# Two slots of SMELU moved to VectorE and GpSimd, one PSUM bank and one output pair moved, loads issued later

## The chip, the cores and the metric

The kernel runs on one core of one Trainium2 chip. The metric is the device time of one execution in microseconds (us). Before the change the median of three runs is 313.86 us (313.83 to 314.38). The profiled execution has a span of 311.6 us from its first to its last instruction.

## What is computed

Sliding-window attention over 8 batches of 8 heads with 576 positions and head size 64, and behind it a two-layer network of 4608 tokens with the activation SMELU between the layers:

```python
scores = scale * np.matmul(q, k.transpose(0, 1, 3, 2))
mask = np.abs(pos[:, None] - pos[None, :]) <= 32
attn = softmax(np.where(mask, scores, -1e9))
x = (attn @ v).transpose(0, 2, 1, 3).reshape(B * S, H * D)     # 4608 x 512
h = x @ w_in                                                   # 4608 x 2048
g = np.where(h >= 1, h, np.where(h <= -1, 0.0, (h + 1) ** 2 / 4))
out = g @ w_out                                                # 4608 x 512
```

So SMELU is zero below -1, the identity above 1, and a quarter of the square of h + 1 between.

## The kernel before

Inputs are float32 in memory and bfloat16 on chip; the sums are float32. Tokens of the network are taken in 18 tiles of 256, and the 2048 hidden columns in 8 blocks of 256. One **slot** `a` of the main loop (L470) is one block of one tile: `t, f = divmod(a, 8)`. In a slot TensorE multiplies `xT` (the transposed output of attention) by a block of `w_in`: 8 matmuls into a tile `hp` of PSUM, 128 partitions by 512 floats, one bank (L492). SMELU of it goes to `gT`, which holds the activations of a tile. Eight slots later blocks of the second layer follow from `gT` and `w_out`: early on in units called `pair` (L440: 8 matmuls of width 256, in an order given by the list `pairs` of slot and unit), later `quarter` (L425: 4 matmuls of width 512).

Attention is spread over the same slots by the table `ev`: transposes of q and k (`tposes`, L323), scores with exponential (`scores`, L211), products with v and the row sums (`sums`, L265). The sums end with two activations on ScalarE and a multiplication on VectorE, which writes `xT`. These multiplications are put off to the next call of `flush`, which comes ahead of and behind SMELU in the next slot (L481, L505). Slot 8 is the first of the second tile of tokens: it reads the columns of `xT` that the multiplications after slots 3, 4 and 5 write (L305 and L308).

The order of work on each engine is that of the program (`manual_schedule`, L73), each engine works its queue in order, and waits between engines go by semaphores that the tile framework places. A tile of a pool with two buffers waits until the last reader of the tile before the last has finished.

**PSUM.** Four pools share the eight banks. `ps_h` has two one-bank buffers for `hp`; `ps_o` has two one-bank buffers for outputs (`op`); `ps_s` and `ps_n` have two banks each for attention. In slots 6 and 7 `hp` is taken from `ps_o` (L486). The buffers of `ps_o` go round: slot 6's `hp`, the output of pairs 0 to 3, then slot 7's `hp`, which so takes the bank of slot 6's. In `ps_h` the tile of slot 8 follows those of slots 4 and 5.

**SMELU** has two forms, both beginning with r = max(0, (h + 1) / 2) on ScalarE (`rr`, L496). In most slots VectorE computes mx = max(h, r) and then g = min(r, 1) * mx (L503, L504). In the slots of `two_on_act` ScalarE also squares r, and VectorE computes g = min(max(h, 1), r squared) (L500, L501). Slots 4 and 5 have the first form.

**Loads.** All loads but the very first go through GpSimd's queue in program order: those of the first batch and `w_in`, the masks' copies, the first half of `w_out` (256 of its 512 columns), then q, k and v of the second batch (`load_rows`, L88; `load_v`, L101), the second half of `w_out`, and q, k and v of the third. A load waits there until the load eight before it has landed. The second batch's q and k are first read by `tposes` in slots 11 and 12 (L412), its v in slot 14. Later batches are loaded by slots (L415 to L421).

**Pairs.** `pairs` puts pair 5, which reads the activations of slots 10 and 11, into slot 13. Slot 12 transposes k of the second batch, ScalarE and VectorE copy it to `kT`, and slot 13 computes scores from that, then pair 5, then the scores of position 13.5.

Of the kernel before, what the change touches and what calls it, by code (L numbers as in the profile page):

```python
# [9 lines left out]
AF = mybir.ActivationFunctionType  # L10
ALU = mybir.AluOpType
# [3 lines left out]
def kernel(  # L15
# [49 lines left out]
    bias = const.tile([128, 192], BF, name="bias")  # L65
# [8 lines left out]
    V, P, A = nc.vector, nc.gpsimd, nc.scalar  # L74
# [19 lines left out]
    def load_nat(b, t):  # L94
        src, dst, nm = ((q, qn, "qn"), (k, kn, "kn"))[t]
        x = dst[b] = nat.tile([128, NU, 2, D], BF, name=nm, tag=nm)
        for h in range(2):
            nc.gpsimd.dma_start(out=x[:, :, h], in_=src[b, NY * h:NY * h + NY].rearrange("y s d -> (y s) d")  # L98
                                .rearrange("(u p) d -> p u d", p=128))

    def load_v(b, n):  # L101
        if b not in vn:
            vn[b] = nat.tile([128, 2 * NC, 2, D], BF, name="vn", tag="vn", bufs=3)
        h, a = divmod(n, 2)
        y = NY * h + 2 * a
        nc.gpsimd.dma_start(out=vn[b][64 * a:64 * a + 64, :, h], in_=v[b, y:y + 2].rearrange("y s d -> (y s) d")  # L106
                            .rearrange("(c r) d -> r c d", r=64))
# [34 lines left out]
    def put(todo):  # L142
        for fn, *x in todo:
            fn(*x)
# [7 lines left out]
    for m, n, x in ((mask4, 8, 128), (mask8, 4, TAIL)):  # L152
        P.tensor_copy(m.rearrange("p (n j) -> p n j", n=n),
                      band[:, :x].rearrange("p (n j) -> p n j", n=1).to_broadcast([128, n, x]))
    put([(load_w_out, 0, 4, 8), (load_w_out, 0, 8, 16)] + [(load_rows, 1, t) for t in range(2)])
    put([(load_v, 1, n) for n in range(4)] + [(load_w_out, 1, 8 * n, 8 * n + 8) for n in range(2)])
    put([(load_rows, 2, t) for t in range(2)] + [(load_v, 2, n) for n in range(4)])


    kT = {}  # L160
# [31 lines left out]
    def xpose(b, t):  # L192

        nc.sync.dma_start_transpose(out=qkT(b, t).rearrange("d (u p) -> d u p", p=128),
                                    in_=(qn, kn)[t][b].rearrange("p u h d -> p (u h d)"))
# [115 lines left out]
    def flush():  # L311
        while muls:
            muls.pop(0)()
# [61 lines left out]

    NB = NT // TB
    NF = DFF // 256
    pairs = [(6, 0), (8, 1), (9, 2), (10, 3), (11, 4), (13, 5), (15, 6), (15, 8), (16, 7), (17, 9)]
    two_on_act = (1, 7, 8, 9, 10, 11, 12)
    ev = {}  # L380

# [34 lines left out]
    for b in range(LONG, B):  # L416
        a = sl[5 * (b - 1) - 7] - 17
# [39 lines left out]
    def run(pos):  # L457
        todo = []
        for fn, *x in ev.get(pos, []):
            if fn is sums:  # L460
                todo.append(sums(*x))
            elif fn is tposes:
                tposes(*x)
            else:
                pool = (x.pop(),) if x[-1] in (ps_s, ps_n, ps_o) else ()
                fn(*x, eng, *pool)
        for end in todo:
            end()

    for a in range(NF * NB + NF):  # L470
        t, f = divmod(a, NF)
        eng = None if a < 14 else V
        post = [x for n, x in pairs if n == a] + [a - NF] * (a >= 2 * NF + 2)
        for b, x in loads.get(a, []):
            if x < 2:
                load_nat(b, x)
            else:
                for n in range(4):
                    load_v(b, n)
        if a == 0 or a > 3:  # L480
            flush()  # L481
        if t < NB:
            if t not in gT:
                gT[t] = gtp.tile([128, 2 * NF, TB], BF, name="gT", tag="gT")
            r0 = TB * t % RING
            if a in (6, 7):  # L486
                hp = ps_o.tile([128, 2, TB], FP, name="hp", tag="op")
            else:
                hp = ps_h.tile([128, 2, TB], FP, name="hp", tag="hp")
            for j in range(2):  # L490
                for n, kk in enumerate((0, 2, 1, 3)):
                    nc.tensor.matmul(hp[:, j], w_in[:, kk, 256 * f + 128 * j:256 * f + 128 * j + 128],  # L492
                                     xT[:, kk, r0:r0 + TB], start=n == 0, stop=n == 3)

            rr = ewp.tile([128, 2, TB], FP, name="rr")
            A.activation(rr, hp, AF.Relu, scale=0.5, bias=0.5)  # L496
            g = gT[t][:, 2 * f:2 * f + 2]
            mx = ewp.tile([128, 2, TB], FP, name="mx")
            if a in two_on_act:
                A.activation(mx, rr, AF.Square)  # L500
                V.scalar_tensor_tensor(g, hp, 1.0, mx, op0=ALU.max, op1=ALU.min)  # L501
            else:
                V.tensor_max(mx, hp, rr)  # L503
                V.scalar_tensor_tensor(g, rr, 1.0, mx, op0=ALU.min, op1=ALU.mult)  # L504
        flush()  # L505
        run(a)
        for x in post:
            (pair if x < 4 * 4 else quarter)(x)
        run(a + 0.5)
        for x in xps.get(a, []):  # L510
            xpose(*x)
# [30 lines left out]
```

The softmax here doesn't subtract the row's maximum and nothing guards it: scores larger than these inputs give would overflow.

## Time and profile before

| what | from the profile |
|---|---|
| span | 311.6 us, 8569 instructions |
| TensorE matmuls, first layer (L492) | 149.3 us, 273 ns each |
| TensorE matmuls, second layer (L432, L448) | 123.0 and 16.5 us |
| SMELU on ScalarE (L496) | 85.7 us, 595 ns each |
| SMELU on VectorE (L503, L504) | 94.5 and 95.3 us, 690 and 696 ns each |
| GpSimd | 73.5 us, nearly all of it issuing loads |
| chain that ended last, by engine | PE 91%, DVE 3%, ACT 3%, issue 3% |
| granted TensorE clock | 0.998 of full speed |

PE is TensorE, PEld its weight loads, DVE VectorE, ACT ScalarE, POOL GpSimd, SP SyncE. L492 is line 492 of the kernel. In a timeline a row gives the start, the duration, engine, line, operation, output and inputs, and in brackets how long the engine sat idle before it and what released it; "x8" is a run of eight instructions. A matmul's recorded duration holds its passage through the array, and the next starts before it ends: eight matmuls of width 256 in a row take 0.87 us in the chain of waits. Engines that are often idle cost nothing unless TensorE waits for them.

### The profile page before, as it was taken

To read this page: it belongs to the slowest core of one execution; us is meant where nothing else is said; L and a number is where in the kernel's file an instruction comes from. 1 tells how busy PE (TensorE), PEld (TensorE's weight loads), DVE (VectorE), ACT (ScalarE), POOL (GpSimd) and SP (SyncE) were. 2 spreads that over 40 slices of the span, in tenths; PEclk is the share of its full clock that TensorE was granted. 3 is DMA by queue.
4 is the path that set the end of the run, shared out by engine and by line. 5 is a ranking of instruction groups with operands and counts; after the bars stand their busy time and mean duration, and the time that the engine had idled before them with its cause. 6 is when DMAs were issued, how large, how long until landed. Compare 5 with 4: busy or idle time off the path is not lost.

```text
span 311.6 us, 8569 instructions
## 1 busy us (share of the span) xinstructions
PE 297.6 (95%) x3669; PEld 207.2 (66%) x3706; DVE 244.9 (79%) x381; ACT 195.3 (63%) x323; POOL 73.5 (24%) x89
## 2 busy tenths in 40 slices
PE   8997989999999999999999999999999999999995
PEld 3566868886666666666666666666666666666652
DVE  4287558888888888888888888888888888888760
ACT  3686876776765766567656666566676666554431
POOL 8898344643061223040504000000000000000000
PEclk9999999999999999999999999999999999999999
DMA  9999999999999999597998592005501100110111
GB/s 151 183 198 199 175 214 177 173 164 167 168 176 131 112 187 162 62 112 153 160 95 81 65 154 70 34 36 113 111 34 36 37 34 36 37 36 34 52 51 67
DMA packets 124118, 34.54 MB, mean 111 GB/s; under 512 B 108208, under 2 KB 119728, under 8 KB 124080
## 3 DMA queue, kind: packets, MB, share of 16 engines
q0 software_dynamic: 94736, 18.06, 75.5%
q1 hardware_dynamic: 29200, 15.63, 20.9%
q8 instruction: 29, 0.48, 0.6%
q10 hardware_dynamic: 144, 0.29, 0.3%
q14 instruction: 9, 0.07, 0.1%
HBM read 36.70 MB, written 9.44 MB: 148 GB/s over the span
## 4 chain that ended last, share of the span: by engine, by line
PE 91%; DVE 3%; ACT 3%; issue 3%; ACTq 0%
PE hp L492 39%; PE op L432 35%; PE bb L293 6%; PE op L448 4%; PE bb L227 2%; PE z L336 2%; PE tp L187 1%; DVE kT L190 1%; DVE xT L305 1%; ACT rc L300 1%; DVE mx L503 1%; ACT rr L496 1%; ACT lr L299 1%; DVE gT L501 0%; ACT mx L500 0%
## 5 line engine op out<-in xcount | busy, mean ns | idle before, releaser
L492 PE MATMUL hp<-xT,w_in 128*128 128x256 bf16 x1152 | 149.3, 273 | 2.8 <-DVE mx L503 1.9
L496 ACT ACTIVATE rr<-hp 128x512 f32<-128x512 f32 x144 | 85.7, 595 | 88.3 <-PE hp L492 88.2
L492 PEld LDWEIGHTS <-w_in 128*128 128x128 bf16 x1152 | 111.9, 98 | 42.5 <-issue 3.3
L432 PE MATMUL op<-w_out,gT 128*128 128x512 bf16 x477 | 123.0, 379 | 5.1 <-issue 4.9
L503 DVE TENSOR_TENSOR mx<-hp,rr 128x512 f32<-128x512 f32 x137 | 94.5, 690 | 31.8 <-ACT rr L496 29.6
L504 DVE SCALAR_TENSOR_TENSOR gT<-rr,mx 128x512 bf16<-128x512 f32 x137 | 95.3, 696 | 4.7
L432 PEld LDWEIGHTS <-gT 128*128 128x128 bf16 x512 | 47.5, 98 | 36.8
L235 ACT ACTIVATE pt<-bb 128x1024 bf16<-128x1024 f32 (+1 forms) x33 | 32.8, 1002 | 5.3 <-PE bb L227 3.8
L106 POOL DMA_DIRECT2D vn<-in_v_dram x32 | 27.3, 868 | 34.1 <-PE bb L227 31.5
L305 DVE TENSOR_TENSOR xT<-bb,rc 128x512 bf16<-128x512 f32 (+1 forms) x32 | 21.1, 658 | 10.1 <-ACT rc L300 9.6
L437 ACT COPY osb<-op 128x512 f32<-128x512 f32 x32 | 18.6, 583 | 11.5 <-PE op L432 11.1
L300 ACT ACTIVATE rc<-lr 128x512 f32<-128x512 f32 (+2 forms) x40 | 23.5, 587 | 1.3
L98 POOL DMA_DIRECT2D qn<-in_q_dram x10 | 12.2, 1221 | 43.5 <-DMA qT<-qn 37.5
L299 ACT ACTIVATE lr<-bb 128x512 f32<-128x512 f32 (+2 forms) x40 | 22.0, 551 | 0.2 <-PE bb L293 0.2
L201 DVE TENSOR_TENSOR pt<-pt,mask 128x1024 bf16<-128x1024 bf16 (+1 forms) x33 | 20.3, 614 | 0.0
L293 PE MATMUL bb<-pt,ones 64*64 64x256 bf16 (+3 forms) x352 | 19.5, 255 | 0.1
L293 PE MATMUL bb<-pt,vn 64*64 64x128 bf16 (+3 forms) x712 | 18.4, 204 | 0.0
L293 PEld LDWEIGHTS <-vn 64*64 64x64 bf16 x712 | 16.7, 107 | 0.2 <-DMA vn<-in_v_dram 0.2
L448 PE MATMUL op<-w_out,gT 128*128 128x256 bf16 x128 | 16.5, 273 | 0.0
L293 PEld LDWEIGHTS <-ones 64*64 64x64 bf16 x352 | 10.2, 105 | 8.5 <-issue 8.4
L98 POOL DMA_DIRECT2D kn<-in_k_dram x10 | 12.1, 1213 | 10.7 <-DMA kT<-kn 3.9
L227 PE MATMUL bb<-qT,kT 64*64 64x128 bf16 (+1 forms) x520 | 13.1, 217 | 0.4 <-DVE kT L190 0.4
(56 smaller groups left out, 118.7 us busy)
## 6 DMA issues: line engine op xcount, KB each, us to landing
out_dram<-osb SPq DMA_DIRECT2D x36, 256.0 KB, 2.3
vn<-in_v_dram POOLq DMA_DIRECT2D x32, 144.0 KB, 8.8
qn<-in_q_dram POOLq DMA_DIRECT2D x10, 288.0 KB, 7.2
kn<-in_k_dram POOLq DMA_DIRECT2D x10, 288.0 KB, 8.0
w_in<-in_moe_w_in_dram POOLq DMA_DIRECT2D x12, 128.0 KB, 5.6
w_out<-in_moe_w_out_dram POOLq DMA_DIRECT2D x3, 512.0 KB, 15.5
qn<-in_q_dram POOLq DMA_DIRECT2D x2, 576.0 KB, 12.8
kn<-in_k_dram POOLq DMA_DIRECT2D x2, 576.0 KB, 13.9
```

What stands on the lines that cost most here:

```text
L98: nc.gpsimd.dma_start(out=x[:, :, h], in_=src[b, NY * h:NY * h + NY].rearrange("y s d -> (y s) d") .rearrange("(u p) d -> p u d", p=128))
L106: nc.gpsimd.dma_start(out=vn[b][64 * a:64 * a + 64, :, h], in_=v[b, y:y + 2].rearrange("y s d -> (y s) d") .rearrange("(c r) d -> r c d", ...
L235: A.activation(p, ps[:, :, :w * n].rearrange(like, y=m), AF.Exp, scale=D ** -0.5)
L293: nc.tensor.matmul(bb[HD[h], a, o + c0:o + c1], ones[HD[a]] if c is None else vn[b][HD[a], c, h], p(a, h), start=n == 0, stop=True, skip_g ...
L299: A.activation(lr[:, :, :D0], bb[:, :, D0:2 * D0], AF.Ln)
L300: A.activation(rc[:, :, :D0], lr[:, :, :D0], AF.Exp, scale=-1.0)
L432: nc.tensor.matmul(o, gT[tt // 2][:, j, 128 * (tt % 2):128 * (tt % 2) + 128], w_out[:, j], start=not done, stop=len(done) == 2 * NF - 1, s ...
L448: nc.tensor.matmul(o[:, tt], gT[p][:, j, 128 * tt:128 * tt + 128], w_out[:, j, 256 * half:256 * half + 256], start=not done, stop=len(done ...
L492: nc.tensor.matmul(hp[:, j], w_in[:, kk, 256 * f + 128 * j:256 * f + 128 * j + 128], xT[:, kk, r0:r0 + TB], start=n == 0, stop=n == 3)
L496: A.activation(rr, hp, AF.Relu, scale=0.5, bias=0.5)
L503: V.tensor_max(mx, hp, rr)
L504: V.scalar_tensor_tensor(g, rr, 1.0, mx, op0=ALU.min, op1=ALU.mult)
```

## The change

Three things. Slot 7's `hp` comes from `ps_h` again, so that it no longer waits for slot 6's bank. Pair 5 goes from slot 13 to slot 12, behind the transposes of k. And slots 4 and 5 compute SMELU without ScalarE: VectorE takes max(h, -1) + 1 from PSUM, GpSimd halves it in place and squares it, and VectorE ends as in the second form. The loads of the second and third batch and of the second half of `w_out`, which stood in GpSimd's queue ahead of the main loop, are issued from slot 4 (q) and slot 5 (all others), each behind GpSimd's two operations of that slot. The aim is to take work off ScalarE in those slots, to take away two waits of TensorE, and to keep the loads in GpSimd's queue from standing ahead of its arithmetic.

```diff
-    put([(load_w_out, 0, 4, 8), (load_w_out, 0, 8, 16)] + [(load_rows, 1, t) for t in range(2)])
-    put([(load_v, 1, n) for n in range(4)] + [(load_w_out, 1, 8 * n, 8 * n + 8) for n in range(2)])
-    put([(load_rows, 2, t) for t in range(2)] + [(load_v, 2, n) for n in range(4)])
+    put([(load_w_out, 0, 4, 8), (load_w_out, 0, 8, 16)])
+    later = {4: [(load_rows, 1, 0)], 5: [(load_rows, 1, 1)] + [(load_v, 1, n) for n in range(4)]}
+    later[5] += [(load_w_out, 1, 8 * n, 8 * n + 8) for n in range(2)]
+    later[5] += [(load_rows, 2, t) for t in range(2)] + [(load_v, 2, n) for n in range(4)]
...
-    pairs = [(6, 0), (8, 1), (9, 2), (10, 3), (11, 4), (13, 5), (15, 6), (15, 8), (16, 7), (17, 9)]
+    pairs = [(6, 0), (8, 1), (9, 2), (10, 3), (11, 4), (12, 5), (15, 6), (15, 8), (16, 7), (17, 9)]
...
-            if a in (6, 7):
+            if a == 6:
                 hp = ps_o.tile([128, 2, TB], FP, name="hp", tag="op")
...
             rr = ewp.tile([128, 2, TB], FP, name="rr")
-            A.activation(rr, hp, AF.Relu, scale=0.5, bias=0.5)
             g = gT[t][:, 2 * f:2 * f + 2]
             mx = ewp.tile([128, 2, TB], FP, name="mx")
-            if a in two_on_act:
+            if a in later:
+                V.tensor_scalar(rr, hp, -1.0, 1.0, op0=ALU.max, op1=ALU.add)
+                P.tensor_scalar(rr, rr, 0.5, None, op0=ALU.mult)
+                P.tensor_mul(mx, rr, rr)
+                V.scalar_tensor_tensor(g, hp, 1.0, mx, op0=ALU.max, op1=ALU.min)
+                put(later[a])
+            else:
+                A.activation(rr, hp, AF.Relu, scale=0.5, bias=0.5)
+            if a in later:
+                pass
+            elif a in two_on_act:
                 A.activation(mx, rr, AF.Square)
                 V.scalar_tensor_tensor(g, hp, 1.0, mx, op0=ALU.max, op1=ALU.min)
```

## The prediction

> **What bounds the kernel now.** The first page gives each engine's share: TensorE is busy 95% of the span, VectorE 79%, ScalarE 63%. A mean hides stages, so next comes the table of stages, cut at 23.6, 45 and 280 us (columns: length, then busy time of PE, PEld, DVE, ACT, POOL, granted clock, DMA share, GB/s):
>
> ```profile
> PE 297.6 (95%) x3669; PEld 207.2 (66%) x3706; DVE 244.9 (79%) x381; ACT 195.3 (63%) x323; POOL 73.5 (24%) x89
> ...
> 23.60:45.00 21.40, 18.61 (x278) 15.25 (x267) 13.55 (x21) 16.09 (x28) 11.83 (x16) 1.00 1.64 194
> 45.00:280.00 235.00, 230.08 (x2890) 162.20 (x2919) 201.40 (x306) 153.32 (x255) 41.08 (x40) 1.00 0.98 105
> ```
>
> From 45 to 280 us TensorE is busy 98% and no wait of over 0.2 us for another engine shows, so a microsecond won or lost on TensorE before 45 us reaches the end whole. All the edits act between 23.6 and 45 us, where TensorE is idle 2.8 us. The waits of TensorE from 20 to 45 us (total, times, longest) name it:
>
> ```profile
> PE hp L492 <- DVE mx L503: 1.9, 1, 1.9
> PE bb L206 <- DVE kT L190: 0.6, 1, 0.6
> PE bb L227 <- DVE kT L190: 0.2, 1, 0.2
> ```
>
> The first is slot 7, as the timelines of VectorE and TensorE show (start, duration):
>
> ```profile
> 24.09 0.62 DVE L305 TENSOR_TENSOR xT<-bb,rc 128x448 bf16<-128x448 f32 x1 [0.54 <-ACT rc L300]
> 24.63 0.68 DVE L503 TENSOR_TENSOR mx<-hp,rr 128x512 f32<-128x512 f32 x1
> 25.35 0.69 DVE L504 SCALAR_TENSOR_TENSOR gT<-rr,mx 128x512 bf16<-128x512 f32 x1
> 25.95 0.62 DVE L305 TENSOR_TENSOR xT<-bb,rc 128x448 bf16<-128x448 f32 x1
> 26.49 0.68 DVE L503 TENSOR_TENSOR mx<-hp,rr 128x512 f32<-128x512 f32 x1
> 27.20 0.69 DVE L504 SCALAR_TENSOR_TENSOR gT<-rr,mx 128x512 bf16<-128x512 f32 x1
> 27.81 0.55 DVE L308 TENSOR_TENSOR xT<-bb,rc 128x384 bf16<-128x384 f32 x1
> 28.28 0.68 DVE L503 TENSOR_TENSOR mx<-hp,rr 128x512 f32<-128x512 f32 x1
> ...
> 26.07 1.04 PE L448 MATMUL op<-w_out,gT 128*128 128x256 bf16 x8
> 29.01 1.91 PE L492 MATMUL hp<-xT,w_in 128*128 128x256 bf16 x16 [1.91 <-DVE mx L503]
> ```
>
> VectorE runs without a pause: xT of slot 3, slot 4, xT of slot 4, slot 5, xT of slot 5, slot 6. Slot 7's projection shares a bank with slot 6's and starts when slot 6's max ends (28.96). The 16 matmuls at 29.01 are slots 7 and 8. Starts give VectorE's spacings: 0.54 from xT to the next operation, 0.72 from one to a dependent one, 0.60 from gT to xT, 0.47 from the short xT on.
>
> The other idle time is at slot 13, whose scores wait for the copies of kT:
>
> ```profile
> 40.20 1.05 PE L492 MATMUL hp<-xT,w_in 128*128 128x256 bf16 x8
> 41.90 0.41 PE L206 MATMUL bb<-bias,ident 64*64 64x512 bf16 x4 [0.65 <-DVE kT L190]
> 42.53 0.41 PE L227 MATMUL bb<-qT,kT 64*64 64x128 bf16 x14 [0.18 <-DVE kT L190]
> 42.88 1.05 PE L448 MATMUL op<-w_out,gT 128*128 128x256 bf16 x8
> ```
>
> **What the Trainium skill says.** "VectorE: DVE Perf Modes", section "Why PSUM operands drop a tier": an fp32 PSUM operand holds VectorE to its base rate. The trace agrees for two-input operations: 0.68 us for 512 elements. "SBUF — State Buffer", "Who interferes with whom": VectorE contends with GpSimd where it has two SBUF inputs, not where it has one. The trace agrees: gT from two SBUF tiles took 1.23 us at 20.47, beside GpSimd's mask copies, and 0.69 elsewhere. "TensorE: Matmul & The Clock Gate", "What's actually happening": an idle window of about 3.4 us halves the clock. After 1.9 us of idle the trace shows no slowing; a longer pause of TensorE here it doesn't show.
>
> **GpSimd's prices.** The trace has GpSimd's copies:
>
> ```profile
> 19.76 0.29 POOL L151 COPY band<-band 64x128 bf16<-64x128 bf16 x1
> L153 POOL COPY mask<-band 128x1024 bf16<-128x1024 bf16 x1 | 1.0, 1038 | 0.1
> L153 POOL COPY mask<-band 128x384 bf16<-128x384 bf16 x1 | 1.0, 967 | 0.0
> ```
>
> 289 ns for 128 elements and 1038 for 1024 give 0.84 ns an element and 0.18 us fixed. For 512 with one input that is 0.61 us. The trace has no two-input GpSimd operation. Low bound: the same 0.61. For the other, "GPSIMD Engine Reference", "Elementwise — side-by-side cycle accounting", gives 2.6 cycles an element at 1.2 GHz: an estimate of 1.11 + 0.14 = 1.25 us, which I take. The leg L of a slot, from the end of its first VectorE operation to the start of its last, is 0.05 + 0.61 + 0.06 + 1.25 + 0.05 = 2.0 us (hops of about 0.05 as from GpSimd's step to ident, 3.03 to 3.07). With one-input rates for both L is 1.4; with the two-input price for both, 2.7.
>
> **The change, part by part.**
>
> *SMELU of slots 4 and 5.* Two ScalarE activations go (0.58 each). ScalarE waits 2.59 us soon after (to 30.08), so this gives nothing. VectorE keeps two operations a slot, but now GpSimd's two stand between them, and VectorE's queue is in order: behind the waiting last operation of slot 4 stand xT of slot 4, all of slot 5, xT of slot 5 and slot 6. Slot 8's projection needs both xT. The ends, from the spacings above:
> - first operation of slot 4: 24.63 to 25.30 (still behind xT of slot 3). gT4 starts 25.30 + L = 27.3, ends 28.0.
> - xT4 at 27.9, first operation of slot 5 at 28.45 to 29.1, gT5 at 27.11 + 2L = 31.1, ends 31.8.
> - xT5 ends 28.26 + 2L = 32.3; slot 6's two and gT7 follow, at +0.47, +0.72, +0.60, +0.69 from xT5's start: gT7 ends 30.19 + 2L = 34.2.
>
> *Bank of slot 7.* It now takes slot 4's bank, so it starts at gT4's end, 28.05, not at 29.01: one of the 1.9 us is won. Slot 8 takes slot 5's bank and needs xT5: it starts at 28.30 + 2L = 32.3 (29.97 before). Its block of 0.98 and pair 1 of 0.87 follow (durations of the chain of waits). Slot 9 takes slot 7's bank, which gT7 frees at 34.25. In the chain of waits slot 9 began at 31.79. So TensorE stands 34.25 − 31.79 = **2.5 us later** (2L − 1.56). From there ScalarE and VectorE keep up as before, with a slot every 1.74 us.
>
> *Pair of slot 12.* Pair 5's 0.98 moves ahead of slot 13, into time in which TensorE waits for kT. In the old clock: pair 5 40.20 to 41.18, slot 13 to 42.05, scores end at 42.95 as before (kT still sets it), the second scores follow at once, slot 14 starts at 43.52 and not 44.49. The second sums then wait for the second exponential (42.99 + 0.92 + 1.02 = 44.93), and slot 15 starts at 45.40, not 46.32: **−0.92**. Pair 5 reads gT of slots 10 and 11, done a slot earlier.
>
> *Loads.* qn of the second batch is issued behind slot 4's product (27.3, not 23.64), kn behind slot 5's (31.1, not 24.38). I cost this at nothing: the DMA engines are full, and GpSimd's waits show w_out landing at 30.7, qn at 33.5, kn at 36.5, so both are issued before the engines come to them. Their first readers are at 36.09 and 39.07 and move later.
>
> Sum: +2.48 − 0.92 = +1.56: 313.86 + 1.56 = **315.4**.
>
> **The rivals.**
> - *GpSimd's leg is short and the mended bank and pair win.* Net is 2L − 2.48, zero at L = 1.24. With both operations at 0.29, the shortest compute row of GpSimd, L is 0.74: −1.0, 312.9. For it: the 1024-element copy ran beside a contending VectorE operation, so its rate may be too high. Against: the 0.29 is for 128 elements of 2 bytes, and here they are 512 of 4 with two reads in the product.
> - *About the same.* The product runs at one-input rate, L = 1.4: +0.3, 314.1. For it: both inputs are one tile. Against: the skill's price.
> - *Worse.* Both at the two-input price, L = 2.7: +2.8, 316.7. With the forecast's L, TensorE is idle 28.9 to 32.3, 3.4 us, just at the skill's window; a halved clock would add about 0.9 for each of two blocks, less slot 9's slack: near 317. Against: the window must be wholly idle.
>
> **How the numbers follow.** Forecast 0.63, short leg 0.10, same 0.12, worse 0.15. The range leaves out the short leg and the far end of the worst case: 314.0 to 317.0. Faster 0.10, within 0.2% 0.12, slower 0.78.
>
> **What would show it.** In the new profile: GpSimd rows of about 0.6 and 1.25 us; VectorE idle about 2 us twice, released by GpSimd; slot 7 at about 28; slot 8 at about 32 released by xT of slot 5; no wait for kT of over 0.5 us before slot 13's scores; TensorE full after. It is wrong if GpSimd's two operations take under 1.1 us together, if qn or kn lands after its transposes are due, or if VectorE's later work doesn't queue behind the last operation of slots 4 and 5.

## The result and the profile after

The changed kernel takes 319.50 us (median of 4 runs, 318.83 to 319.67), the kernel before 313.87: a ratio of 1.0172, with an interval of 1.0154 to 1.0190. The change makes the kernel 5.6 us slower; 1.6 us slower was forecast. The profiled execution has a span of 316.8 us, 5.2 more than before, and was the shortest of the four runs.

TensorE's waits from 20 to 46 us in the changed kernel (total, times, longest; line numbers are up to 10 higher than before, so L493 is the first layer's matmul):

```profile
PE hp L493 <- DVE xT L309: 4.0, 1, 4.0
PE hp L493 <- DVE gT L503: 1.9, 1, 1.9
```

The 1.9 us for slot 6's max are gone, and so are the 0.8 us for kT: slot 13's scores, now at 47.98, wait for nothing that shows. In their place stand 1.9 us of slot 7 for slot 4's last operation, and 4.0 us of slot 8 for xT of slot 5. VectorE's timeline shows what holds those:

```profile
24.72 0.68 DVE L500 TENSOR_SCALAR rr<-hp 128x512 f32<-128x512 f32 x1
28.23 0.69 DVE L503 SCALAR_TENSOR_TENSOR gT<-hp,mx 128x512 bf16<-128x512 f32 x1 [2.83 <-POOL mx L502]
28.84 0.61 DVE L306 TENSOR_TENSOR xT<-bb,rc 128x448 bf16<-128x448 f32 x1
29.37 0.68 DVE L500 TENSOR_SCALAR rr<-hp 128x512 f32<-128x512 f32 x1
32.86 0.69 DVE L503 SCALAR_TENSOR_TENSOR gT<-hp,mx 128x512 bf16<-128x512 f32 x1 [2.81 <-POOL mx L502]
33.47 0.55 DVE L309 TENSOR_TENSOR xT<-bb,rc 128x384 bf16<-128x384 f32 x1
```

This is the order of the kernel before with two holes of 2.8 us in it, both ended by GpSimd. GpSimd's timeline for the same time:

```profile
25.58 1.50 POOL L501 TENSOR_SCALAR rr<-rr 128x512 f32<-128x512 f32 x1 [2.39 <-DVE rr L500]
27.16 1.04 POOL L502 TENSOR_TENSOR mx<-rr 128x512 f32<-128x512 f32 x1
...
30.23 1.48 POOL L501 TENSOR_SCALAR rr<-rr 128x512 f32<-128x512 f32 x1 [1.23 <-DVE rr L500]
31.79 1.04 POOL L502 TENSOR_TENSOR mx<-rr 128x512 f32<-128x512 f32 x1
```

The halving takes 1.5 us, longer than the square (1.04), though it has one input. Last, TensorE (slots 7 and 8, pair 1, slots 9 and 15), slots 9 and 15 of the kernel before, and the changed kernel's table of stages of 2 us, whose column before the last two is the granted clock:

```profile
29.07 1.03 PE L493 MATMUL hp<-xT,w_in 128*128 128x256 bf16 x8 [1.88 <-DVE gT L503]
34.07 1.86 PE L493 MATMUL hp<-xT,w_in 128*128 128x256 bf16 x8 [3.97 <-DVE xT L309]
35.73 1.91 PE L449 MATMUL op<-w_out,gT 128*128 128x256 bf16 x8
37.44 1.16 PE L493 MATMUL hp<-xT,w_in 128*128 128x256 bf16 x8
...
51.40 1.05 PE L493 MATMUL hp<-xT,w_in 128*128 128x256 bf16 x8
```

```profile
31.63 1.04 PE L492 MATMUL hp<-xT,w_in 128*128 128x256 bf16 x8
...
46.25 0.94 PE L492 MATMUL hp<-xT,w_in 128*128 128x256 bf16 x7
```

```profile
30.00:32.00 2.00, 0.11 (x1) 0.00 (x0) 0.05 (x1) 1.23 (x2) 1.69 (x2) 0.71 1.02 157
32.00:34.00 2.00, 0.00 (x0) 0.00 (x0) 1.14 (x3) 0.00 (x0) 2.00 (x3) 0.50 0.77 129
34.00:36.00 2.00, 1.93 (x10) 1.33 (x10) 1.91 (x4) 0.00 (x0) 2.00 (x3) 0.50 0.80 84
```

In the pause the granted clock falls to half, and slot 8 and pair 1 each run in about 1.9 us instead of 1.04. Cut more finely, the table shows one stretch at half, from 30.86 to 37.69: 6.83 us, of which TensorE works in 3.62. Slot 9 starts at 37.44; before it started at 31.63.

### The profile page after: what moved, and what is told of

The parts are those of the page before. It is cut to its first block, busy times and chain, and to the rows that moved or that the text cites. A ratio compares the mean times of both kernels' runs of the same rounds, so it can differ in the third digit from the quotient of the medians.

```text
span 316.8 us, 8573 instructions
## 1 busy us (share of the span) xinstructions
PE 299.4 (95%) x3669; PEld 208.2 (66%) x3706; DVE 244.0 (77%) x381; ACT 194.2 (61%) x321; POOL 78.8 (25%) x93
## 4 chain that ended last, share of the span: by engine, by line
PE 90%; ACT 3%; issue 3%; DVE 2%; POOL 2%; POOLq 0%; DVEq 0%; ACTq 0%
PE hp L493 38%; PE op L433 34%; PE bb L294 6%; PE op L449 5%; PE bb L228 2%; PE z L337 2%; PE tp L188 2%; POOL rr L501 1%; ACT pt L236 1%; POOL mx L502 1%; DVE xT L306 1%; ACT rc L301 1%; ACT lr L300 1%; DVE rr L500 0%; ACT rr L506 0%
## 5 line engine op out<-in xcount | busy, mean ns | idle before, releaser
L493 PE MATMUL hp<-xT,w_in 128*128 128x256 bf16 x1152 | 150.4, 274 | 6.5 <-DVE xT L309 4.0
L493 PEld LDWEIGHTS <-w_in 128*128 128x128 bf16 x1152 | 112.3, 98 | 46.9 <-issue 7.3
L506 ACT ACTIVATE rr<-hp 128x512 f32<-128x512 f32 x142 | 84.5, 595 | 95.0 <-PE hp L493 94.2
L513 DVE TENSOR_TENSOR mx<-hp,rr 128x512 f32<-128x512 f32 x135 | 93.1, 690 | 31.6 <-ACT rr L506 29.6
L514 DVE SCALAR_TENSOR_TENSOR gT<-rr,mx 128x512 bf16<-128x512 f32 x135 | 93.6, 693 | 4.6
L433 PEld LDWEIGHTS <-gT 128*128 128x128 bf16 x512 | 47.5, 98 | 36.8
L449 PE MATMUL op<-w_out,gT 128*128 128x256 bf16 x128 | 17.4, 282 | 0.0
L449 PEld LDWEIGHTS <-gT 128*128 128x128 bf16 x128 | 12.4, 101 | 2.3
```

The costliest lines, as they stand in the source:

```text
L433: nc.tensor.matmul(o, gT[tt // 2][:, j, 128 * (tt % 2):128 * (tt % 2) + 128], w_out[:, j], start=not done, stop=len(done) == 2 * NF - 1, s ...
L449: nc.tensor.matmul(o[:, tt], gT[p][:, j, 128 * tt:128 * tt + 128], w_out[:, j, 256 * half:256 * half + 256], start=not done, stop=len(done ...
```

## The experiments

The theory: VectorE stands in its in-order queue behind GpSimd in slots 4 and 5, TensorE waits for what is queued there, and its clock then falls to half. The rivals: the loads that are issued later; GpSimd's arithmetic beside VectorE; SMELU without ScalarE as such. Each ratio is against runs of the kernel before on the same chip.

| kernel | time, us | ratio to before (interval) |
|---|---|---|
| e1_bank | 312.85 | 0.9965 (0.9951 to 0.9978) |
| e2_pair | 313.01 | 0.9979 (0.9972 to 0.9985) |
| e3_bank_pair | 312.18 | 0.9950 (0.9934 to 0.9966) |
| e4_smelu_loads | 321.63 | 1.0249 (1.0234 to 1.0265) |
| e5_warm | 317.16 | 1.0106 (1.0089 to 1.0123) |
| e6_no_half | 314.07 | 1.0018 (1.0006 to 1.0030) |
| e7_vector_only | 312.79 | 0.9969 (0.9957 to 0.9981) |
| e8_half_tile | 319.10 | 1.0168 (1.0153 to 1.0183) |
| e9_loads_late | 313.68 | 1.0001 (0.9994 to 1.0008) |
| e10_two_op | 316.78 | 1.0086 (1.0062 to 1.0110) |
| e11_reorder | 314.05 | 1.0019 (1.0007 to 1.0031) |

### The parts of the change alone

e1_bank and e2_pair are the kernel before with one line of the change each; e3_bank_pair has both:

```diff
-            if a in (6, 7):
+            if a == 6:
...
-    pairs = [(6, 0), (8, 1), (9, 2), (10, 3), (11, 4), (13, 5), (15, 6), (15, 8), (16, 7), (17, 9)]
+    pairs = [(6, 0), (8, 1), (9, 2), (10, 3), (11, 4), (12, 5), (15, 6), (15, 8), (16, 7), (17, 9)]
```

> The kernel before with slot 7's bank alone changed. Leg theory (the loss is VectorE standing in its queue behind GpSimd in slots 4 and 5): nothing stands there now, so slot 7 follows pair 0 at once (27.1), slot 8 waits for xT of slot 5 (28.4 instead of 29.97), slot 9 for the gT of slot 7 (30.3 instead of 31.8): -1.45 us, 312.4. Rival (slot 7's bank only moves the wait to xT of slot 5 and to the gT of slot 7, and later slots take it back): within 0.5 us of before.

> The kernel before with pair 5 alone moved to slot 12. The prediction's step says -0.9 us; the changed kernel's trace has slots 9 to 15 shorter by 0.66 than before. So -0.7 to -0.9, 313.0 to 313.2. Rival (the copies of kT move later with it): no change.

> Bank and pair together, no SMELU on GpSimd and loads as before. Both waits are taken away in different slots, so they add: -2.1 to -2.4 us, 311.5 to 311.8, if all of the loss is in the SMELU of slots 4 and 5. Rival (slots 11 to 13 can't use time that comes earlier, as the loads of the second batch then land too late): less than the larger one of the two alone.

They gave −1.0, −0.8 and −1.6 us against 313.82: each does what it is for, and together nearly their sum. The pair came out as expected, the bank and both together smaller. In e1_bank slot 9 starts at 30.48, 1.15 us earlier than before: the expected 1.45 had taken slot 9 of before from the chain of waits (31.8, not 31.63), and VectorE began slot 4 there 0.13 later. In e3_bank_pair TensorE waited 1.0 us for a piece of `w_in` in slot 3 in the profiled run, so some of the shortfall of that run lies ahead of the change. e3_bank_pair is the fastest of all kernels here, 0.5% below the kernel before and 2.3% below the changed one.

e4_smelu_loads is the changed kernel with these two lines put back.

> SMELU of slots 4 and 5 and the late loads alone, bank and pair as before. Leg theory with half clock: slot 7 now waits for slot 6's max, which ends at 34.6 in the changed kernel (29.0 before): +5.6 us, and after a pause of 7 us TensorE runs at half clock for about two blocks, +1.9: 321.3. Without the half clock: 319.5. If the bank mended in the changed kernel gained nothing there, the time is that of the changed kernel less or plus 0.7: 320.2.

It gave 321.63, with a half clock in its profile (TensorE waits 6.8 us for slot 6's max). So the whole loss comes with the SMELU of slots 4 and 5 and the loads behind it, and the other two parts take 2.1 us of it back.

### Loads or arithmetic

e9_loads_late keeps the kernel before in everything but the loads, and puts GpSimd's two operations on a spare tile, so that the loads are as late as in the changed kernel and VectorE waits for nothing:

```diff
+            if a in later:
+                A.activation(rr, hp, AF.Relu, scale=0.5, bias=0.5)
+                V.tensor_max(mx, hp, rr)
+                V.scalar_tensor_tensor(g, rr, 1.0, mx, op0=ALU.min, op1=ALU.mult)
...
+                P.tensor_scalar(s1, mx, 0.5, None, op0=ALU.mult)
+                P.tensor_mul(s2, s1, s1)
+                put(later[a])
```

> Bank, pair and SMELU as before the change; but in slots 4 and 5 GpSimd does its two operations on a spare tile behind the max of VectorE, and the loads of the second batch stand behind them, as in the changed kernel. VectorE waits for nothing of it. Leg theory: the loads come late as in the changed kernel and nobody waits for them; gT of the slots may run beside GpSimd's reads, up to 0.5 us longer each, in slots whose max sets slot 7: 313.8 to 314.9. Rival (late loads or GpSimd's work beside VectorE are what costs): 316 or more.

No difference: 1.0001. The loads of k were issued at 32.79 (32.78 in the changed kernel), and TensorE shows no wait for them. The late loads cost nothing, and neither does GpSimd's arithmetic as long as nobody waits for it. Where VectorE's gT ran beside it, both took longer, by little: GpSimd's first row 1.99 and 1.76 us instead of 1.5, and slot 6's gT 1.04 us instead of 0.69.

### The leg's length

> The changed kernel without GpSimd's halving in slots 4 and 5 (the activations of these two slots are then squared without the factor). L falls from 2.83 to about 0.18 + 1.04 + 0.03 = 1.25 us. By the leg's sum slot 9 comes 2 x 1.58 = 3.2 us earlier, and TensorE's pause falls to about 2.6 us, without half clock: another 1.4. So 319.5 - 4.6 = 314.9. If only the later loads cost: no change.

```diff
-                P.tensor_scalar(rr, rr, 0.5, None, op0=ALU.mult)
                 P.tensor_mul(mx, rr, rr)
```

> The changed kernel with GpSimd's two operations replaced by one of VectorE, (0.25 r) r, so that a slot has three operations in a row on VectorE and GpSimd only issues loads. L is about 0.75 us: slot 9 comes 2 x 2.08 = 4.2 us earlier and there is no half clock (1.4): 313.9. The loads go out as early as before. If GpSimd's arithmetic isn't the cost, but taking ScalarE out is: over 317.

```diff
-                P.tensor_scalar(rr, rr, 0.5, None, op0=ALU.mult)
-                P.tensor_mul(mx, rr, rr)
+                V.scalar_tensor_tensor(mx, rr, 0.25, rr, op0=ALU.mult, op1=ALU.mult)
```

e6_no_half leaves out the factor 0.5, so it doesn't compute SMELU in these two slots and serves only to price the wait. It gave 314.07 (314.9 expected), e7_vector_only 312.79 (313.9 expected). With a leg of 1.2 us the change is about even, and with VectorE doing all three operations itself it is faster than before. So leaving ScalarE out isn't the cost; the wait is. Both came out about 1 us lower than expected, which fits the larger price of the half clock in the next experiment.

### The half clock

> The changed kernel with 17 matmuls of width 512 on a bank of attention that is free just then, put ahead of slot 8's projection: TensorE works through most of its 4.0 us wait, and nothing waits for them. If half clock after the pause costs 1.4 us (slot 8 and pair 1 took 3.37 us, not 1.85, and slot 9's bank is free at 35.98): -1.4, 318.1. If the two blocks are slow for another reason (reading xT or w_out beside VectorE or the loads): no change or later.

```diff
...
+            if a == 8:
+                keep_warm(17, ps_n, "bb")
```

It gave 317.16, 2.3 us less than the changed kernel, although it does more work. TensorE's timeline of e5_warm from the added matmuls on (16 of the 17 are in the trace), then slot 8, pair 1 and slot 9:

```profile
29.77 3.83 PE L340 MATMUL z<-warm 128*128 128x512 bf16 x16
33.91 1.03 PE L498 MATMUL hp<-xT,w_in 128*128 128x256 bf16 x8 [0.30 <-DVE xT L309]
34.78 1.04 PE L452 MATMUL op<-w_out,gT 128*128 128x256 bf16 x8
35.84 1.03 PE L498 MATMUL hp<-xT,w_in 128*128 128x256 bf16 x8
```

Slot 8 starts where it did within 0.2 us, but it and pair 1 run at full rate, and slot 9 starts 1.93 us behind slot 8, not 3.37. That is the half clock's share: 1.4 us in the profiled runs, as expected, and 2.3 in the medians (the profiled run of the changed kernel was its shortest). e6 and e7 have no half clock in their medians.

In kernels with a shorter pause the clock doesn't fall in every run, which prices it within one kernel. (A mean over the run of 0.995 is what 3.4 us at half come to, the stretch in the trace of e10_two_op below; 0.989 is what 6.8 us come to.) Among the 20 runs of e6_no_half the twelve with a mean granted clock of 0.998 or more took 313.77 to 314.23 us, the eight at 0.992 to 0.995 took 315.01 to 315.53: about 1.4 us. In e11_reorder below, runs at 0.999 to 1.000 took 313.86 to 314.36, at 0.995 315.55 to 316.12, and one at 0.987 took 317.06.

### Why GpSimd's halving takes 1.5 us

> The changed kernel with the halving as a product with a tile of 0.5 instead of with a constant. If GpSimd's operation with a constant is the slow one (1.50 us against 1.04 for the two-input product in the changed kernel's trace), it falls to 1.04 to 1.2: L 2.4, slot 9 0.6 to 0.9 us earlier, and the pause of TensorE falls from 4.0 to 3.2 us, which may or may not bring half clock: 318.7 with it, 317.2 without. If the first operation is slow because it is the first after a pause of GpSimd or because it works in place: no change, 319.5.

```diff
...
-                P.tensor_scalar(rr, rr, 0.5, None, op0=ALU.mult)
+                P.tensor_mul(rr, rr, half_t)
```

The row fell to 1.28 us and the leg to 2.58, but the time stayed at 319.10. TensorE's pause was still 3.7 us. Slot 8 started 0.67 us earlier than in the changed kernel, but the clock was now at half for slot 8, pair 1, slot 9 and most of pair 2, so the gain went back:

```profile
36.77 1.91 PE L495 MATMUL hp<-xT,w_in 128*128 128x256 bf16 x8
38.47 1.38 PE L451 MATMUL op<-w_out,gT 128*128 128x256 bf16 x8
```

The stretch at half is as long as in the changed kernel, 6.83 us (32.33 to 39.16), but it begins later, and TensorE works in 5.76 us of it instead of 3.62. The expectation of 318.7 held for the leg and missed this.

> The kernel before with nine GpSimd operations on 128 x 512 elements behind the last SMELU, while VectorE is idle: fp32 square of one tile, times a constant, product of two tiles, copy, times a constant again, the same in place, times and plus a constant, copy to bf16, bf16 times a constant in place. If an operation with a constant is the slow form: 1.4 to 1.5 for each of those and 1.0 to 1.3 for products and copies. If being in place is what made the changed kernel's 1.50: only the in-place rows are slow. If it was the first after a pause: only the first row is. Time about as before, as the rows lie beside TensorE's last blocks.

```diff
...
+    P.tensor_mul(mo, m0, m0)
+    P.tensor_scalar(mo, m0, 0.5, None, op0=ALU.mult)
+    P.tensor_mul(mo, m0, half_t)
+    P.tensor_copy(mo, m0)
...
+    P.tensor_scalar(mo, mo, 0.5, None, op0=ALU.mult)
+    P.tensor_scalar(mo, m0, 0.5, 1.0, op0=ALU.mult, op1=ALU.add)
...
+    P.tensor_scalar(mb, mb, 0.5, None, op0=ALU.mult)
```

GpSimd's timeline in m1_pool_rows, in the order of the diff:

```profile
304.07 1.04 POOL L519 TENSOR_TENSOR mo<-m 128x512 f32<-128x512 f32 x1 [133.44 <-DVE m L518]
305.20 1.50 POOL L520 TENSOR_SCALAR mo<-m 128x512 f32<-128x512 f32 x1
306.78 1.27 POOL L521 TENSOR_TENSOR mo<-m,half_t 128x512 f32<-128x512 f32 x1
308.11 0.61 POOL L522 COPY mo<-m 128x512 f32<-128x512 f32 x1
...
310.38 1.49 POOL L524 TENSOR_SCALAR mo<-mo 128x512 f32<-128x512 f32 x1
311.95 0.62 POOL L525 TENSOR_SCALAR mo<-m 128x512 f32<-128x512 f32 x1
...
313.21 1.49 POOL L527 TENSOR_SCALAR mb<-mb 128x512 bf16<-128x512 bf16 x1
```

The starts confirm the durations: each row starts about 0.1 us behind the end of the one before. Being in place doesn't matter (1.50 and 1.49), nor does being first. Times a constant takes 1.5 us; times a constant **plus** a constant takes 0.62, like a copy. So, other than I had expected, it isn't the constant that is slow, but the form with one step. A bfloat16 tile times a constant took 1.49 as well. (The expectation that the time would stay was wrong: the nine rows run to 314.7 us of the profile, while TensorE's last matmul ends at 308.4, and the one run took 318.01.)

### The leg with the shorter form, and VectorE's order

> The changed kernel with GpSimd's halving written with a second step, times 0.5 plus 0, the form that took 0.62 us in m1_pool_rows where times 0.5 alone took 1.49. L falls to 0.18 + 0.62 + 0.08 + 1.04 + 0.03 = 1.95 us, the leg that the prediction had assumed. By the leg's sum slot 9 comes 1.8 us earlier: 317.7 if TensorE still falls to half clock in the pause of about 3.3 us, 315.4 if not. If the short row of m1 was short for another reason (its place in the row of operations): no change, 319.5.

```diff
-                P.tensor_scalar(rr, rr, 0.5, None, op0=ALU.mult)
+                P.tensor_scalar(rr, rr, 0.5, 0.0, op0=ALU.mult, op1=ALU.add)
```

```profile
25.77 0.61 POOL L501 TENSOR_SCALAR rr<-rr 128x512 f32<-128x512 f32 x1 [1.68 <-DVE rr L500]
26.47 1.04 POOL L502 TENSOR_TENSOR mx<-rr 128x512 f32<-128x512 f32 x1
```

The row fell to 0.61 us in place and VectorE's holes from 2.8 to 1.94. The median is 316.78; one run at a mean granted clock of 1.000 took 315.45, the three at 0.995 took 316.71 to 317.07. With the leg that the prediction assumed and no half clock, the kernel takes the time that it forecast, as far as one run can say.

> The kernel of e10_two_op with the same instructions in another order on VectorE: slot 4's last operation behind slot 5's first, slot 5's behind slot 6's two, so that xT of slots 4 and 5 doesn't stand behind GpSimd. If the queue is what costs, slot 8 now waits only for slot 5's gT at about 30.7 (34.07 in the changed kernel) with a pause of under 2 us and no half clock, and slot 9 starts at about 32.5: 313.9. If GpSimd's duration costs whatever the order: as e10_two_op.

```diff
                 V.tensor_scalar(rr, hp, -1.0, 1.0, op0=ALU.max, op1=ALU.add)
+                while last:
+                    last.pop(0)()
...
-                V.scalar_tensor_tensor(g, hp, 1.0, mx, op0=ALU.max, op1=ALU.min)
+                last.append(lambda g=g, hp=hp, mx=mx: V.scalar_tensor_tensor(g, hp, 1.0, mx, op0=ALU.max, op1=ALU.min))
...
+            if a == 6:
+                while last:
+                    last.pop(0)()
```

314.05, as expected (313.9), and 2.7 us less than e10_two_op with the same instructions. About 1.4 of this is the order itself: at a mean clock of 0.999 or more it took 313.86 to 314.36, e10_two_op 315.45 in its one such run. The rest is that the clock fell in 5 of its 20 runs, and in 3 of 4 of e10_two_op. VectorE's hole ahead of slot 4's last operation shrank to 0.77 us, since xT of slot 4 and slot 5's first operation ran in it. So the queue's order costs, beside GpSimd's speed: the shorter row had taken as much, 2.7 us, off the changed kernel.

The profiled run was the slowest of the 20 (317.06), and it shows the clock falling in short pauses (slots 7 and 8, pair 1, slot 9):

```profile
28.29 1.03 PE L494 MATMUL hp<-xT,w_in 128*128 128x256 bf16 x8 [0.99 <-DVE gT L506]
31.19 1.89 PE L494 MATMUL hp<-xT,w_in 128*128 128x256 bf16 x8 [1.87 <-DVE gT L506]
32.87 1.91 PE L450 MATMUL op<-w_out,gT 128*128 128x256 bf16 x8
34.58 1.91 PE L494 MATMUL hp<-xT,w_in 128*128 128x256 bf16 x8
```

e11_reorder still doesn't beat e3_bank_pair, which leaves the two slots to ScalarE.

## Why the prediction was wrong

Its side was right, its size was not: +1.6 forecast, +5.6 measured, outside the range of 314.0 to 317.0. On the profiled runs the terms can be summed to the end. Slot 9 starts 5.8 us later than before and slot 15 5.15 us later (46.25 and 51.40), and the spans differ by 5.2.

- **What bounds the kernel: right.** From 45 us on nothing was won back: 5.15 us at slot 15 are 5.2 at the end.
- **VectorE's queue behind the leg: right.** The predicted sum for slot 8, 28.30 + 2L, gives 33.96 with the measured L of 2.83, and it started at 34.07. e10_two_op and e11_reorder confirm both halves of it, the leg's length and the order.
- **The leg L: the term that was mis-sized.** Taken as 2.0 us, with 2.7 as its worst; it measured 2.83 and 2.81. The failed step is "For 512 with one input that is 0.61 us": the rate of a copy, right for a copy (0.61 in m1_pool_rows), was taken for a multiplication with one constant, which takes 1.5. The square was taken too long: the estimate of 1.25 came from the 2.6 cycles an element that the Trainium skill gives in "GPSIMD Engine Reference", section "Elementwise — side-by-side cycle accounting", and it measured 1.04 for one tile with itself; for two different tiles it measured 1.27, close to that estimate. The hop from VectorE to GpSimd was 0.18 us, not 0.05. The leg comes twice: 2 x 0.81 = 1.6 us (the sum was made with 2.02).
- **The half clock: named, and left out of the sum. The second step that failed.** The Trainium skill, "TensorE: Matmul & The Clock Gate", section "What's actually happening", speaks of an idle window of about 3.4 us, and the prediction leaned on "the window must be wholly idle". The runs differ from that: in the profiled run of e11_reorder the clock fell in a pause of 1.87 us, with a block of 1 us and a pause of 0.99 ahead of it. In e6_no_half the longest pause was 1.9 us in its one profile, which is at full clock, and 8 of its 20 runs had a reduced clock. In the changed kernel it cost 1.46 us in the profiled run (slot 9 at 37.44, while its bank was free at 35.98), and by the medians of e5_warm 2.3. The rival's price was near: 0.9 for each of two blocks, less a slack that by its own times was 0.1.
- **Bank of slot 7: right in place.** It follows slot 4's last operation as predicted, which came 0.9 later; slot 7 starts at 29.07, not at 28.05. Alone the edit is worth 1.0 us (e1_bank). Beside the SMELU it is worth more: without bank and pair e4_smelu_loads takes 2.1 us longer than the changed kernel, of which the pair is 0.7 to 0.8.
- **Pair of slot 12: right in kind, somewhat less in size.** −0.92 forecast, −0.8 alone in e2_pair, −0.66 in the changed kernel, where slot 9's block still ran partly below full clock (0.12 of the difference).
- **The loads at nothing: right**, shown by e9_loads_late.

Together: +1.56 forecast, +1.62 of leg, +1.46 of half clock, +0.26 of the pair's smaller gain, +0.09 because VectorE began that much later, and 0.16 because slot 9 of before was read from the chain of waits (31.79) and not from the timeline (31.63): 5.15 us. The remaining 0.5 us to the medians' 5.6 is the difference between the profiled run and the others. Their mean clocks are 0.989 twice and 0.987, against 0.989, so a longer stretch at half shows in one of them at most; whether more work fell into it, as in e8_half_tile, can't be told without their traces, so it stays open.

Of the rivals, the "worse" one came nearest, but its 2.7 us leg and its half clock were priced one without the other; they came together, because a longer leg is what makes the longer pause.

## What to carry to other kernels

When an operation moves to another engine, look at what is queued behind the instruction that waits for it: the same instructions in an order that lets independent work pass cost 2.7 us less here, the clock's share included. Price an unfamiliar form of an operation by a row of its own, not by the rate of a similar one, and let the range hold the case that it is more than twice as slow. And add to a new pause of TensorE what its clock does afterwards. Shortening such a pause can gain next to nothing, if the stretch at half only falls on more work.

## What the runs showed of the hardware

- GpSimd's multiplication with one constant takes 1.49 to 1.50 us for 128 x 512 elements, in float32 and bfloat16, in place or not; with a second constant added it takes 0.62, a copy 0.61, a square 1.04, a product of two tiles 1.27 (m1_pool_rows, VectorE idle).
- TensorE's clock fell to half in pauses whose longest was 1.87 us (e11_reorder) to 6.8 us (e4_smelu_loads); with the shorter ones only in some runs of a kernel; what decides it is open. In the kernel before, with a single pause of 1.9 us, no run shows a mean clock below 0.998. The stretch at half lasted 3.42 us in the trace of e10_two_op, and 6.8 in those of the changed kernel, e4_smelu_loads, e8_half_tile and e11_reorder. It cost 1.4 to 3 us a time, and shortening the pause from 4.0 to 3.7 us gained 0.4 us in the medians (e8_half_tile). Seventeen matmuls on a free bank took it away (e5_warm).
